# Where the projections of a backward kernel put their results: two PSUM banks instead of four, and one group made a stage earlier

## The chip, the core and the metric

The kernel runs on one core of one Trainium2 chip. The metric is the device time of one execution in microseconds (us); lower is better. The five engines are named as the profile names them: PE (TensorE, with its weight loads shown apart as PEld), DVE (VectorE), ACT (ScalarE), POOL (GpSimd) and SP (SyncE, which here only issues DMAs). PSUM is the memory that PE writes its results to; this kernel uses all eight of its banks.

## The reference: a gated mix of attention and a GLU, forward and backward

```python
x = A_x                                         # 1 x 2048 x 512
g = _sigmoid((x * gate_w).sum(-1, keepdims=True))
a = _A_ref(x, A_wqkv, A_wo)                     # 32 heads of 16, each row sees the last 256 keys
b = _B_ref(x, B_W_gate, B_W_up, B_W_down)       # relu(x Wg) * (x Wu), then Wd; inner width 1376
return g * a + (1 - g) * b
...
_out, _vjp = jax.vjp(_f, A_x, A_wqkv, A_wo, B_W_gate, B_W_up, B_W_down, gate_w)
_grads = _vjp(grad_out)
return (_out0, *[jnp.asarray(_g) for _g in _grads])
```

The outputs are the mix itself and its gradients with respect to the input and the six weights, in bfloat16.

## The kernel before: three stages, and an order of work that is written out by hand

**First stage** (lines 190 to 498): the GLU branch. Steps run over 11 blocks of 128 inner columns (`fc`) and, inside, over 4 groups of 512 tokens (`tg`), 44 steps in all (`N1`). A step makes gate and up products, the backward product `dh`, and six steps later (`at(6)`) the weight gradients (`weights`, lines 393 to 427). The loop runs 8 iterations past the last step, to empty this pipeline. In that tail the attention's first projections are slipped in: `first` holds the parts of token group 0, one popped per iteration (lines 489 to 493).

**Second stage** (lines 500 to 981): the attention, forward and backward together. The outer loop `c` runs over 4 chunks of 8 heads, the inner loop `j` over 16 blocks of 128 query tokens; for each query block up to three key blocks are visited, the diagonal one (role "d"), the one before (role "m") and the farthest (role "f"), each for two halves of four heads. One such visit is a unit; there are 90 units per chunk and 360 in all, and the loop variable `n` counts them. The order of instructions is written by hand (`manual_schedule`): every engine does its instructions in the order in which this loop issues them.

For unit `n`, `front` (line 666) makes the scores `ST` on PE, ACT takes their exponential into `Pu` (line 682), POOL masks it for roles d and f (lines 684, 687). `front_dp` (line 690) makes `dPT` on PE, and one step later `gradp` (line 698) multiplies the two on DVE. Three steps later `rowsum` (line 703) sums on PE into `BA`. Then the two results are turned over, `flip` (line 721): either by a DMA transpose issued on SP (line 729, all of role d, most of role m in the first three chunks), or by eight PE transposes into a PSUM tile `pt` and one copy on ACT or DVE (lines 734 to 741). The turned pairs feed `cd_piece` (line 524), which adds up the gradients of K and V in `CD`. `small_ops` (line 744) is the row arithmetic on POOL.

Beside the units, three kinds of work are put in by a running `credit` for PE's time (lines 866 to 965). First, `project_parts` (line 118) makes Q, dO, K, V for the next group of 512 tokens: the list `prq` of six parts (Q, dO, the DMA transpose `rows` of both, K, V, and the transposes `ptp` of K and V). Each of the four matmul parts has one PSUM tile `pp` of a whole bank, four matmuls and one reading copy; after Q and dO, four DVE copies `spread` (line 512) lay them out by heads. Second, `grad_parts` (line 613) makes the gradient of the projection weights of the chunk before: four sums per chunk, each a PSUM tile `wps` that stays open for four pieces of four matmuls (lines 621 to 632). Third, `late` and `early` issue loads and DMA transposes on SP for the last stage; `early` (line 784) holds one step that only makes a list and then four DMA transposes of the first 256 tokens' results.

**The PSUM banks of this stage.** Pool `ps` has four banks under the tag "M" and one for `CD`; pool `psr` has two under the tag "TR" and one for `BA`. Before, `ST`, `dPT`, `pp` and `wps` share the four "M" banks (line 511 sends the projections there), and `pt` and `ptp` have the two "TR" banks.

**SBUF pairs.** A d or m pair stays in a buffer `PPd` or `PPm`, three of each (line 677), until its DMA or PE transposes have read it. In the last chunk the pairs of query blocks 12 and 14 of role d are kept in `PPm` as well (line 675).

**Third stage** (lines 983 to 1090): for 8 pairs of token blocks, the output and the gradient of x, by long rows of 512-column matmuls. Its first groups use `T0` (from `early`), `f0` and `f1` (from `early_f`).

Of the kernel before, what the change touches and what calls it, by code (L numbers as in the profile page):

```python
# [11 lines left out]
BF = mybir.dt.bfloat16  # L12
F32 = mybir.dt.float32
# [9 lines left out]
def kernel(  # L23
# [88 lines left out]
    if True:  # L112
        HH = HG // 2
        proj = {}
        groups = [(c, tg) for c in range(DC) for tg in range(NTG)]
        PENG = ("dvs", "dvs")

        def project_parts(c, tg):
            t4 = {}
            proj[(c, tg)] = t4  # L120
            pj = pjA if (c * NTG + tg) % 3 == 0 else pjs["b"]

            def mm(nm, which, eng):
                ps, tag, bufs, _, _ = pools["now"]
                pp = ps.tile([P, TGW], F32, tag=tag, bufs=bufs, name="pp")
                for cd in range(DC):
                    if which < 3:
                        nc.tensor.matmul(pp[:], lhsT=w_p[c][:, cd, which * P:(which + 1) * P], rhs=x_T[tg][:, cd, :],  # L128
                                         start=(cd == 0), stop=(cd == DC - 1))
                    else:  # L130
                        nc.tensor.matmul(pp[:], lhsT=w_p[c][:, cd, 3 * P:4 * P], rhs=da_T[tg][:, cd, :],
                                         start=(cd == 0), stop=(cd == DC - 1))
                if nm in ("Q", "dO"):
                    if nm == "Q":
                        t4["z"] = pjA.tile([P, 2, TGW], BF, tag="zT", name="zT")
                    dst = t4["z"][:, ("Q", "dO").index(nm), :]
                else:
                    dst = pjA.tile([P, TGW], BF, tag="T", bufs=2, name=f"{nm}T")[:]
                if nm == "Q" and (c, tg) == groups[1]:
                    nc.scalar.mul(dst, pp[:], scale)  # L140
                elif nm == "Q":
                    nc.vector.tensor_scalar(dst, pp[:], scale, None, op0=ALU.mult)
                else:
                    evac(dst, pp[:], eng)
                t4[nm] = dst
                if nm in ("Q", "dO"):
                    if c == 0 and tg == 0:
                        w = ("Q", "dO").index(nm)
                        for k in range(NP):
                            rows = slice(32 * k, 32 * k + 32)  # L150
                            evac(zt[0][rows, w, k, :, :], dst[rows, :].rearrange("p (k q) -> p k q", k=TPG),
                                 (("dve", "act")[w] if k % 2 else "dve"))
                else:
                    for k in range(2):
                        t4[f"{nm}{k}"] = pj.tile([P, TGW], BF, tag=f"{nm}{k}", name=f"{nm}{k}")
                        if PENG[k] == "act":
                            nc.scalar.mul(t4[f"{nm}{k}"][:], pp[:], par[:, k:k + 1])
                        elif PENG[k] == "dve":
                            nc.vector.tensor_scalar(t4[f"{nm}{k}"][:], pp[:], par[:, k:k + 1], None, op0=ALU.mult)
                        else:  # L160
                            nc.vector.tensor_scalar(t4[f"{nm}{k}"][:], dst[:], par[:, k:k + 1], None, op0=ALU.mult)

            def tr(a_nm, b_nm):
                _, _, _, ps, trt = pools["now"]
                pt = ps.tile([P, 2, TPG, P], BF, tag=trt, bufs=2, name="ptp")
                for a, nm in enumerate((a_nm, b_nm)):
                    for k in range(TPG):
                        nc.tensor.transpose(pt[:, a, k, :], t4[nm][:, k * P:(k + 1) * P], ident[:])
                return pt

            def tr_rows():
                rows = pjA.tile([P, 2, TPG, P], BF, tag="rows", bufs=2, name="rows")
                nc.sync.dma_start_transpose(out=rows[:].rearrange("p a t d -> p (a t) d"),
                                            in_=t4["z"][:].rearrange("p a s -> p (a s)"))
                t4["rows"] = rows

            def tr_kv():
                kv = pj.tile([P, TPG, HG, 34], BF, tag="KV1", name="KV1")
                nc.gpsimd.memset(kv[:, :, :, 0:1], -1.0)
                nc.gpsimd.memset(kv[:, :, :, Dh + 1:Dh + 2], 1.0)  # L180
                pt = tr("K", "V")
                v = lambda a: pt[:, a, :, :].rearrange("p k (h d) -> p k h d", h=HG)
                nc.vector.tensor_scalar(kv[:, :, :, 1:1 + Dh], v(0), scale, None, op0=ALU.mult)
                nc.vector.tensor_copy(kv[:, :, :, Dh + 2:2 * Dh + 2], v(1))
                t4["kv"] = kv

            return [lambda: mm("Q", 0, "dve"), lambda: mm("dO", 3, "dve"), tr_rows, lambda: mm("K", 1, "act"),
                    lambda: mm("V", 2, "act"), tr_kv]

    with ExitStack() as p1, tc.manual_schedule():  # L190
# [248 lines left out]
        for n in range(N1 + 8):  # L439
# [51 lines left out]
            for _ in range({N1 + 1: 2, N1 + 2: 0}.get(n, 1)):  # L491
                if first:
                    first.pop(0)()
            z = n - DA0 - NT - 2
            if z == 0:
                load_w(0)
# [4 lines left out]
    if True:  # L501
# [6 lines left out]
        ps = pps.enter_context(tc.tile_pool(name="attps", bufs=2, space=PSUM))  # L508
        ppr = ExitStack()
        psr = ppr.enter_context(tc.tile_pool(name="attpr", bufs=2, space=PSUM, side="right"))  # L510
        pools["now"] = (ps, "M", 4, psr, "TR")
        def spread(gi, k):
            rows = slice(32 * k, 32 * k + 32)
            nc.vector.tensor_copy(zt[gi % ZB][rows, :, k, :, :].rearrange("p w t q -> p w (t q)"),
                                  proj[groups[gi]]["z"][rows, :, :])

        P2 = {}
        RQ = {}
        CDs = {}
# [93 lines left out]
        def grad_parts(c, tail=False):  # L613
            out = []
            hold = {}

            def store(part, ws):
                to = out_2[part * P:(part + 1) * P, :].rearrange("p (a n) -> p a n", a=3)[:, :, c * P:(c + 1) * P]
                return lambda: nc.sync.dma_start(to, ws[:])

            def piece(part, t0, first, last):
                if first:
                    hold[part] = ps.tile([P, 3, P], F32, tag="M", bufs=4, name="wps")
                wps = hold[part]
                for t in range(t0, t0 + 4):
                    nc.tensor.matmul(wps[:], lhsT=x_r[:, t, part * P:(part + 1) * P], rhs=sts[c][:, t, 0:3, :],  # L626
                                     start=first and t == t0, stop=last and t == t0 + 3)
                if not last:
                    return None
                ws = (S2["t6"] if tail else gwp).tile([P, 3, P], BF, tag="ws", bufs=5 if tail else 2, name="ws")  # L630
                evac(ws[:], wps[:], "act" if not tail or part % 2 else "dve")
                return store(part, ws)

            if tail:
                for a, b in ((0, NT - 4), (NT - 4, NT)):
                    out += [(p, t0, t0 == 0, t0 + 4 == NT) for p in range(DC) for t0 in range(a, b, 4)]
                return [lambda a=a: piece(*a) for a in out]
            for part in range(DC):
                for t0 in range(0, NT, 4):
                    out.append((lambda part=part, t0=t0, f=(t0 == 0), l=(t0 + 4 == NT): piece(part, t0, f, l), t0 + 4 < NT))  # L640
            return out
# [24 lines left out]
        def front(u):  # L666
# [5 lines left out]
            nc.tensor.matmul(ST[:], lhsT=KTt[:, ksl], rhs=z[:, 0, :, jl, :], start=True, stop=True)  # L672
            if not u.own:
                if u.half == 0:
                    kind = "m" if u.c == DC - 1 and u.j > 11 and u.j % 2 == 0 else u.role
                    tag = f"PP{kind}"
                    pairs[(u.c, u.j, u.kb)] = wk.tile([P, 2, 2, HH, P], BF, tag=tag, bufs=3, name=tag)
                u.PP = pairs[(u.c, u.j, u.kb)][:, u.half, :, :, :]
# [42 lines left out]
        def flip(u):  # L721
# [3 lines left out]
            if u.dma:  # L725
# [5 lines left out]
                for b in range(2)[hs]:  # L731
                    P2[(u.c, u.j, u.kb, b)] = P2[key][:, b, :, :, :]
                return
            eng = ("act", "dve")[copier["i"] % 2]
            copier["i"] += 1
            pt = psr.tile([P, 2, HH, P], BF, tag="TR", name="pt")
            for a, src in enumerate((u.Pu, u.Pd)):
# [99 lines left out]
        with tc.manual_schedule():  # L837
# [37 lines left out]
            while n <= NU + LAG or ev or cdq or bgq:  # L875
                now = ev.pop(n, [])
                u = units[n] if n < NU else None
                if u is not None:
# [2 lines left out]
                        sts[u.c] = st.tile([P, NT, 4, P], BF, tag="rows_st", name="rows_st")  # L881
                    if u.first and u.j % TPG == 0:
                        if gi + 1 < len(groups):
                            prq = project_parts(*groups[gi + 1])
                            due = n + sum(2 * min(3, j + 1) for j in range(u.j, u.j + TPG)) - 3
                            if gi + 2 == len(groups):
                                due -= 10
# [72 lines left out]
                if late and (u is None or u.c == 0 or (n % 12 == 1 and 3 <= u.j <= 8 if u.c < DC - 1 else  # L960
                                                       n % 4 == 1 and 1 < u.j < 10 or n % 2 and u.j > 9)):
                    late.pop(0)()
                if early and n % 3 == 0 and (len(early) > 4 or u is None or u.j >= 11):
                    early.pop(0)()
                credit = max(-1.0, min(1.2, credit))
                for eng, f in now:
# [154 lines left out]
```

## Time and profile before

| | us |
|---|---|
| median of 3 runs | 921.34 |
| the runs | 919.93, 921.34, 921.94 |
| the profiled execution, its own time | 921.62 |
| its span, first to last instruction | 919.9 |
| outside the span | 1.7 |
| PE busy in the span | 903.5 (98%) |
| DVE, ACT, POOL busy | 511.5, 437.8, 493.6 |
| first attention unit (its `ST`) starts | 249.74 |
| unit 18, the first of token group 1 | 270.76 |
| chunks 1, 2 and 3 start | 356.36, 473.90, 591.44 |
| the last unit's `ST` | 715.02 |

How to read it: all times inside the execution count from the start of the span. The PE busy time counts each matmul with a modelled end; a matmul of 512 columns is shown as 379 ns although the next one starts some 215 ns after it, so that short waits do not appear as idle time. The spacing of the starts in the timeline shows them.

### The profile page before, as it was taken

How to read it: one execution, taken by the hardware profiler on the slowest of the kernel's cores; microseconds unless marked ns; L12 is line 12 of the kernel's file. 1: busy time of each engine (PE TensorE's matmuls, PEld its weight loads, DVE VectorE, ACT ScalarE, POOL GpSimd, SP SyncE). 2: the span in 40 equal slices, each digit the busy share in tenths (PEclk: the TensorE clock that was granted, in tenths of full speed). 3: DMA queues.
4: the chain of work that ended last, by engine and by line, in shares of the span. 5: the costliest groups of instructions: out<-in, count | busy, mean ns of one | idle time of the engine just before them, and what ended most of it. 6: DMA issues, size and time to landing. Idle time of an engine off the chain costs nothing.

```text
span 919.9 us, 26221 instructions
## 1 busy us (share of the span) xinstructions
PE 903.5 (98%) x10711; PEld 569.7 (62%) x10711; DVE 511.5 (56%) x957; ACT 437.8 (48%) x773; POOL 493.6 (54%) x937
## 2 busy tenths in 40 slices
PE   9999999999999999999999999999998999999998
PEld 6556656556657776667666677766776644444445
DVE  4333344334288887668876687777786222222223
ACT  7322222222367777667776677766687300011111
POOL 4544445445277777767787677775777311111111
PEclk9999999999999999999999999999999999999999
DMA  9988889999699999998999989999999799777741
GB/s 303 193 195 188 190 179 215 221 222 194 159 164 157 179 182 187 191 164 149 171 196 187 162 158 182 184 179 185 181 187 197 184 255 234 183 188 184 184 93 46
DMA packets 505576, 169.07 MB, mean 184 GB/s; under 512 B 433456, under 2 KB 504336, under 8 KB 505456
## 3 DMA queue, kind: packets, MB, share of 16 engines
q1 hardware_dynamic: 484816, 145.51, 85.8%
q10 hardware_dynamic: 19008, 17.31, 6.9%
q0 software_dynamic: 1632, 4.59, 1.4%
q8 instruction: 83, 1.36, 0.6%
q14 instruction: 37, 0.30, 0.1%
HBM read 32.28 MB, written 36.24 MB: 74 GB/s over the span
## 4 chain that ended last, share of the span: by engine, by line
PE 79%; POOL 7%; DVE 4%; DMA 4%; issue 2%; ACT 2%; SPq 1%; ACTq 0%; POOLq 0%; DVEq 0%
PE dxps L1046 8%; PE ST L672 7%; PE dPT L696 7%; PE wps L403 7%; PE pt L739 5%; PE wps L626 4%; PE dxps L1050 4%; PE bps L1019 4%; PE pp L128 4%; PE CD L533 3%; PE BA L710 3%; PE dps L405 3%; PE ups L354 3%; PE gps L354 3%; PE dhps L354 3%
## 5 line engine op out<-in xcount | busy, mean ns | idle before, releaser
L696 PE MATMUL dPT<-z,V 128*128 128x512 bf16 x360 | 136.4, 379 | 3.7 <-ACT PPm L682 2.4
L672 PE MATMUL ST<-z,K 128*128 128x512 bf16 x360 | 136.3, 379 | 2.0 <-ACT PPm L682 0.3
L684 POOL TENSOR_SCALAR_AFFINE_SELECT PPd<-PPd 128x512 bf16<-128x512 bf16 x124 | 79.1, 638 | 106.9 <-ACT PPd L682 106.1
L701 DVE TENSOR_TENSOR Pd<-Pu,dPT 128x512 bf16<-128x512 bf16 x117 | 80.1, 684 | 64.7 <-POOL Pu L687 62.7
L368 POOL TENSOR_TENSOR hT<-rg,upm 128x512 bf16<-128x512 bf16 x44 | 51.5, 1171 | 116.1 <-DVE upm L366 90.0
L403 PE MATMUL wps<-dgu_r,x_r 128*128 128x256 bf16 (+1 forms) x704 | 103.9, 270 | 0.9 <-DVE wst L74 0.8
L701 DVE TENSOR_TENSOR PPd<-PPd,dPT 128x512 bf16<-128x512 bf16 x124 | 84.4, 680 | 15.5 <-POOL PPd L684 14.8
L403 PEld LDWEIGHTS <-x_r 128*128 128x128 bf16 x704 | 68.3, 98 | 31.9 <-issue 1.8
L682 ACT ACTIVATE PPd<-ST 128x512 bf16<-128x512 f32 x124 | 74.4, 600 | 27.3 <-PE ST L672 26.5
L682 ACT ACTIVATE PPm<-ST 128x512 bf16<-128x512 f32 x119 | 71.2, 601 | 29.9 <-PE ST L672 25.8
L682 ACT ACTIVATE Pu<-ST 128x512 bf16<-128x512 f32 x117 | 70.2, 600 | 28.9 <-PE ST L672 28.8
L701 DVE TENSOR_TENSOR PPm<-PPm,dPT 128x512 bf16<-128x512 bf16 x119 | 79.4, 667 | 6.5 <-POOL PPm L684 4.1
L687 POOL TENSOR_SCALAR_AFFINE_SELECT Pu<-Pu 128x512 bf16<-128x512 bf16 x112 | 73.7, 658 | 16.2 <-ACT Pu L682 15.6
L1026 ACT COPY a_sb<-aps 128x512 f32<-128x512 f32 x16 | 9.4, 586 | 151.4 <-issue 137.6
L366 DVE SCALAR_TENSOR_TENSOR upm<-rg,ups 128x512 bf16<-128x512 bf16 x44 | 30.1, 684 | 80.6 <-PE ups L354 44.2
L360 ACT ACTIVATE rg<-gps 128x512 bf16<-128x512 f32 x44 | 26.3, 598 | 88.4 <-PE gps L354 33.1
L405 PE MATMUL dps<-db_r,h_r 128*128 128x512 bf16 x176 | 66.7, 379 | 0.0
L72 ACT COPY p<-pt 128x1024 bf16<-128x1024 bf16 x62 | 63.0, 1016 | 5.2 <-PE dPT L696 0.4
L378 POOL TENSOR_TENSOR dgu<-dh_sb,rg 128x512 bf16<-128x512 bf16 x44 | 57.2, 1301 | 5.1 <-ACT dh_sb L374 5.1
L1032 POOL DMA_DIRECT2D out_dram<-o_sb x16 | 8.7, 542 | 89.2 <-DVE o_sb L1030 82.7
L128 PE MATMUL pp<-x,p 128*128 128x512 bf16 x192 | 49.0, 378 | 1.5 <-ACT PPm L682 1.0
L626 PE MATMUL wps<-rows_st,x_r 128*128 128x384 bf16 x256 | 50.3, 325 | 0.0
(193 smaller groups left out, 2362.3 us busy)
## 6 DMA issues: line engine op xcount, KB each, us to landing
dqkvo_d<-rows_st SPq DMA_DIRECT2D x15, 512.0 KB, 4.2
hT_d<-hT ACTq DMA_DIRECT2D x44, 128.0 KB, 2.5
dgT_d<-dgu ACTq DMA_DIRECT2D x44, 128.0 KB, 3.0
duT_d<-dgu ACTq DMA_DIRECT2D x44, 128.0 KB, 3.0
duT_g<-duT_d SPq DMA_DIRECT2D x8, 640.0 KB, 5.6
gt<-hT_d SPq DMA_DIRECT2D x7, 640.0 KB, 6.0
dgT_g<-dgT_d SPq DMA_DIRECT2D x7, 640.0 KB, 5.3
out_dram<-wst SPq DMA_DIRECT2D x20, 128.0 KB, 2.7
```

The source lines that it names most:

```text
L128: nc.tensor.matmul(pp[:], lhsT=w_p[c][:, cd, which * P:(which + 1) * P], rhs=x_T[tg][:, cd, :], start=(cd == 0), stop=(cd == DC - 1))
L354: nc.tensor.matmul(out[:], lhsT=w(c), rhs=x(c), start=(c == 0), stop=(c == DC - 1))
L403: nc.tensor.matmul(acc["w"][:, c, 0:2 * nw], lhsT=x_r[:, t, c * P:(c + 1) * P], rhs=k.dgu_r[:, :, i, s0:P], start=(go_ and c % 2 == 0), st ...
L405: nc.tensor.matmul(acc["d"][:], lhsT=k.h_r[:, i, :], rhs=db_r[:, t, :], start=go_, stop=no_)
L626: nc.tensor.matmul(wps[:], lhsT=x_r[:, t, part * P:(part + 1) * P], rhs=sts[c][:, t, 0:3, :], start=first and t == t0, stop=last and t == ...
L672: nc.tensor.matmul(ST[:], lhsT=KTt[:, ksl], rhs=z[:, 0, :, jl, :], start=True, stop=True)
L682: nc.scalar.activation(u.Pu[:], ST[:], ACT.Exp)
L684: nc.gpsimd.affine_select(out=u.Pu[:], in_=u.Pu[:], compare_op=ALU.is_ge, fill=0.0, base=0, pattern=[[0, HH], [1, P]], channel_multiplier=-1)
L687: nc.gpsimd.affine_select(out=u.Pu[:], in_=u.Pu[:], compare_op=ALU.is_ge, fill=0.0, base=-1, pattern=[[0, HH], [-1, P]], channel_multiplier=1)
L696: nc.tensor.matmul(u.dPT[:], lhsT=VTt[:, ksl], rhs=z[:, 1, :, jl, :], start=True, stop=True)
L701: nc.vector.tensor_tensor(out=u.Pd[:], in0=u.Pu[:], in1=u.dPT[:], op=ALU.mult)
L1046: nc.tensor.matmul(to, lhsT=src[:, fc, lsl], rhs=W6[(wt, fc)][:, cols], start=(fc == 0 and wt == "Wg"), stop=False)
```

## The change

The four parts of the change, as the code has them:

1. In the second stage `project_parts` takes its PSUM tiles from "TR" of `psr` instead of "M" of `ps`, and so do the `wps` sums of chunks 0 and 1 (made while chunks 1 and 2 run). The sums of chunks 2 and 3 stay in "M".
2. Q, dO and their `rows` transpose of token group 1 are made in the tail of the first stage, at its iterations `N1 + 4`, `N1 + 5` and `N1 + 6`, with the four `spread` copies right behind dO. `spread` moves up to where it can be called there, and the pool of the K and V buffers is looked up when a part runs. The attention's first group then has only K, V and their transposes left to put in.
3. In chunk 0 the copies of `pt` go ACT, DVE, ACT in turn, instead of ACT, DVE.
4. In the last chunk only query block 12's d pair is kept in `PPm`; block 14's goes to `PPd`. The list step of `early` may run from block 9 on, its four DMA transposes from block 14 on at even `n`; before, list and transposes ran at every third `n`, the transposes from block 11 on.

```diff
+        def spread(gi, k):
+            ...
         def project_parts(c, tg):
             t4 = {}
             proj[(c, tg)] = t4
-            pj = pjA if (c * NTG + tg) % 3 == 0 else pjs["b"]
+            pj = lambda: pjA if (c * NTG + tg) % 3 == 0 else pjs["b"]
...
+                    elif nm == "dO" and (c, tg) == groups[1]:
+                        for k in range(NP):
+                            spread(1, k)
...
             for _ in range({N1 + 1: 2, N1 + 2: 0}.get(n, 1)):
                 if first:
                     first.pop(0)()
+            if n == N1 + 3:
+                second = project_parts(*groups[1])
+            if n in (N1 + 4, N1 + 5, N1 + 6):
+                second.pop(0)()
...
-        pools["now"] = (ps, "M", 4, psr, "TR")
-        def spread(gi, k):
-            ...
+        pools["now"] = (psr, "TR", 2, psr, "TR")
...
             def piece(part, t0, first, last):
                 if first:
-                    hold[part] = ps.tile([P, 3, P], F32, tag="M", bufs=4, name="wps")
+                    own, tag, bufs = (ps, "M", 4) if c + 2 >= DC else (psr, "TR", 2)
+                    hold[part] = own.tile([P, 3, P], F32, tag=tag, bufs=bufs, name="wps")
...
-                    kind = "m" if u.c == DC - 1 and u.j > 11 and u.j % 2 == 0 else u.role
+                    kind = "m" if u.c == DC - 1 and u.j == 12 else u.role
...
-            eng = ("act", "dve")[copier["i"] % 2]
+            eng = ("act", "dve", "act")[copier["i"] % 3] if u.c == 0 else ("act", "dve")[copier["i"] % 2]
...
-                            prq = project_parts(*groups[gi + 1])
+                            prq = project_parts(*groups[gi + 1]) if gi else second
...
-                if early and n % 3 == 0 and (len(early) > 4 or u is None or u.j >= 11):
+                if early and (u is None or n % 2 == 0 and u.j >= (9 if len(early) > 4 else 14)):
                     early.pop(0)()
```

More of the change, by code (lines that the diff above doesn't have):

```diff
@@ L116 @@
         PENG = ("dvs", "dvs")
+        def spread(gi, k):
+            rows = slice(32 * k, 32 * k + 32)
+            nc.vector.tensor_copy(zt[gi % ZB][rows, :, k, :, :].rearrange("p w t q -> p w (t q)"),
+                                  proj[groups[gi]]["z"][rows, :, :])
         def project_parts(c, tg):
@@ L152, in mm @@
                                  (("dve", "act")[w] if k % 2 else "dve"))
+                    elif nm == "dO" and (c, tg) == groups[1]:
+                        for k in range(NP):
+                            spread(1, k)
                 else:
                     for k in range(2):
-                        t4[f"{nm}{k}"] = pj.tile([P, TGW], BF, tag=f"{nm}{k}", name=f"{nm}{k}")
+                        t4[f"{nm}{k}"] = pj().tile([P, TGW], BF, tag=f"{nm}{k}", name=f"{nm}{k}")
                         if PENG[k] == "act":
@@ L177, in tr_kv @@
             def tr_kv():
-                kv = pj.tile([P, TPG, HG, 34], BF, tag="KV1", name="KV1")
+                kv = pj().tile([P, TPG, HG, 34], BF, tag="KV1", name="KV1")
                 nc.gpsimd.memset(kv[:, :, :, 0:1], -1.0)
@@ L510 @@
         psr = ppr.enter_context(tc.tile_pool(name="attpr", bufs=2, space=PSUM, side="right"))
-        pools["now"] = (ps, "M", 4, psr, "TR")
-        def spread(gi, k):
-            rows = slice(32 * k, 32 * k + 32)
-            nc.vector.tensor_copy(zt[gi % ZB][rows, :, k, :, :].rearrange("p w t q -> p w (t q)"),
-                                  proj[groups[gi]]["z"][rows, :, :])
+        pools["now"] = (psr, "TR", 2, psr, "TR")
         P2 = {}
```

## The prediction, as it went on record

> **What bounds the kernel now.** I read the page's first and fourth parts, then the windows by stage, then the chain of waits and the timeline of the attention stage.
>
> ```profile
> span 919.9 us, 26221 instructions
> ...
> PE 903.5 (98%) x10711; PEld 569.7 (62%) x10711; DVE 511.5 (56%) x957; ACT 437.8 (48%) x773; POOL 493.6 (54%) x937
> ...
> PE 79%; POOL 7%; DVE 4%; DMA 4%; issue 2%; ACT 2%; SPq 1%; ACTq 0%; POOLq 0%; DVEq 0%
> ```
>
> PE is busy almost throughout and makes up 79% of the chain that ended last. What can be won is therefore the time in which PE starts nothing. Idle time hides most of that, because a matmul's end is modelled: the chain shows four 512-column matmuls as 0.86 us, 0.215 each, where the groups give 379 ns. So I went through PE's rows of the timeline from 249 to 710 us and took from each start-to-start distance what the matmul costs back to back (512 columns 0.215 us, 384 columns 0.163, a 128-column transpose 0.056, the small sums 0.025). The useful work comes to 437.1 us, the lost time to 22.9 us. All that follows is a share of these 22.9.
>
> The dearest single loss is near the end of the attention. The chain of waits there:
>
> ```profile
> 697.93 5.94 DMA p2d<-PPm
> 703.95 0.61 ACT PPm L682
> 704.60 0.38 PE dPT L696
> ```
>
> and the windows around it (PE busy, PEld, DVE, ACT, POOL, granted clock, DMA share, GB/s):
>
> ```profile
> 702.00:704.60 2.60, 0.23 (x3) 0.00 (x1) 0.18 (x1) 0.65 (x2) 0.00 (x0) 1.00 0.55 150
> ...
> 706.00:708.00 2.00, 2.00 (x28) 1.45 (x25) 1.40 (x4) 1.66 (x3) 1.75 (x5) 0.52 0.91 193
> 708.00:709.50 1.50, 1.50 (x28) 0.95 (x27) 0.53 (x1) 0.79 (x2) 1.18 (x4) 0.50 0.94 253
> ```
>
> The exponential of block 14's d pair must have a PPm buffer, and the next one free is that of block 12's pair, whose DMA transpose lands at 703.86. PE stands for 2.37 us, and then runs 3.5 us at half clock (0.52 and 0.50), 1.75 us more.
>
> The commonest loss is around a projection. The timeline (start, us, engine, line):
>
> ```profile
> 303.29 1.03 PE L131 MATMUL pp<-d,p 128*128 128x512 bf16 x4
> ...
> 304.36 0.69 DVE L74 CAST zT<-pp 128x512 bf16<-128x512 f32 x1
> 304.37 0.38 PE L696 MATMUL dPT<-z,V 128*128 128x512 bf16 x1
> ...
> 304.96 0.68 DVE L701 TENSOR_TENSOR PPd<-PPd,dPT 128x512 bf16<-128x512 bf16 x1
> 305.10 0.38 PE L672 MATMUL ST<-z,K 128*128 128x512 bf16 x1
> ```
>
> ST at 305.10 could not start until the cast had left pp's bank at 305.05; the eight BA sums before it were through at about 304.99. 21 of the 60 projection tiles in the attention are followed by such a wait.
>
> **End of the attention (block 14's pair to PPd).** PPd's three buffers then hold the pairs of blocks 11, 13 and 14, and 14 takes the one that block 10 left; that transpose was issued at 680.49 and landed at 686.20, 18 us before the need. Most that can come back: 2.37 + 1.75 = 4.1. Next late there is ACT, which in 712 to 716 is busy 3.89 of 4.00 us without holding PE up. I take 3.8.
>
> By the Trainium skill ("TensorE: Matmul & The Clock Gate", Part 1: The HAM clock gate) the clock halves only after an idle window of about 3.4 us. The 2.37 us of this trace were enough, so the trace decides; by the page the idle time alone, 2.4, would come back.
>
> **Projections out of the M banks.** From 271 us on (groups 2 to 15 in their making, 56 tiles) the lost time is 2.4 us before pp itself (mostly for an exponential to leave a bank), 2.4 before ST and dPT while a pp is open, and 2.3 before an ST that the copy out of pp released: 7.1 us, 0.13 a tile. With four banks for ST and dPT alone none of these waits has its cause left, but the DVE casts (0.69) and ACT casts (0.59) still stand in the same queues ahead of the products and exponentials that free the banks. Between 0 and 7.1 I take 60%, 4.3.
>
> What it costs in TR: I laid the life of every pt (129, mean 1.87 us from first transpose to end of copy), ptp (1.50), pp (1.72) and wps (6.88) of the trace over two banks. At no start are two others still alive; the tightest distances are 0.14 us (a wps at 396.2 and 513.7), and 0.57 for a pt behind a pt with wps open (397.3, 514.8). So 0; if the cover goes, see the third rival.
>
> **wps of chunks 0 and 1 to TR.** While a wps is open 0.97 us are lost before ST and dPT, in three chunks; two of them move: at most 0.65, I take 0.3.
>
> **Token group 1 in the first stage.** The tail before:
>
> ```profile
> 249.52 0.38 PE L405 MATMUL dps<-db_r,h_r 128*128 128x512 bf16 x1
> 249.74 0.38 PE L672 MATMUL ST<-z,K 128*128 128x512 bf16 x1
> 249.77 0.48 ACT L72 CAST wst_end<-wps 128x384 bf16<-128x384 f32 x1 [8.52 <-PE wps L403]
> ...
> 250.28 0.56 DVE L74 CAST wst_end<-wps 128x384 bf16<-128x384 f32 x1 [3.91 <-ACT wst_end L72]
> ```
>
> PE has no gap there (9.40 of 9.50 us busy from 240 to 249.5), so eight matmuls put the first ST off by 2 x 0.865 = 1.73, to about 251.5. Moved with them: the Q copy on ACT (0.60), covered, as ACT stands idle for 8.52; dO's cast (0.69) and four spreads (0.49 each, 1.96) on DVE, which come behind wst_end and before the first product, and hold that back to about 3.4 us after its ST instead of 2.3; one SP transpose (1.84), behind four stores (1.99) and ahead of the first p2d. The attention gives the 1.73 back, and the 2.65 on DVE. K, V and ptp move to n = 0, 2, 4, so units 5 to 17 run bare: they took 15.55 us with 2.2 of projection in them, and units 30 to 37, bare, 1.0 each, so 13.3. Units 0 to 4 take some 5.9 instead of 5.5 to n = 5. So 251.5 + 5.9 + 13.3 = 270.7, against 270.76. I take 0; the lost 4.4 us of this group and the 1.73 bound it at -2 and +2.
>
> **Copies in chunk 0.**
>
> ```profile
> L72 ACT COPY p<-pt x62: 1012/1012/1042, 262.8 to 718.7; 128x1024 bf16<-128x1024 bf16 x62
> L74 DVE COPY p<-pt x50: 676/684/692, 268.1 to 669.8; 128x1024 bf16<-128x1024 bf16 x50
> ```
>
> Of 28 copies 19 instead of 14 are ACT's: 5 x 1.01 = +5.1 on ACT, 5 x 0.68 = -3.4 on DVE. In chunk 0 ACT is busy 79.6 and DVE 86.6 of 106.7 us; they come level. 0, within 1 either way.
>
> **early later.** Its four transposes took SP 2.38 + 1.24 + 1.30 + 2.28 = 7.2 us between 682 and 697, ahead of block 12's and 13's p2d and the Wd loads. They now stand before block 14's and 15's p2d, f1 and wo. Cover: block 14's pair is used at 727.50, block 15's landed at 721.40 and is used at 728.30 (PE has 24 and more wps matmuls between), T0 is first read by aps at 733.81, f1 landed at 724.40 and is read at 734.67. If all 7.2 fell on block 15, with the attention 3.8 earlier: 724.8 against a need at 724.5, 0.3 lost. I take 0, at most 1.
>
> **Sum.** 3.8 + 4.3 + 0.3 = 8.4 off the profiled execution's 921.62 (span 919.9 and 1.7 around it): 913.2. That execution lies 0.28 above the median of the runs shown, 921.34; I put the forecast at 913.2. Bounds: all losses back 4.1 + 7.1 + 0.65 + 2 + 1 = 14.9, 906.7; only a part of the end back, 921.
>
> **Rivals.**
> 1. *The waits come back on ACT and DVE.* For: DVE is busy 70.0 of 85.6 us in the rest of chunk 0, and its largest wait, Pd for POOL's Pu, 62.7 us, stays. ST and dPT then wait for the late product instead of the bank, and only the end is gained: 921.6 - 3.8 = 917.8. Against: 2.3 us of the waits name pp's own copy. Chance 0.16.
> 2. *The change does not do what it says.* The first stage pays 1.73 and the DVE spreads delay the first units by the 2 bound; the end gains 3.8: 921.6 + 2 + 1 - 3.8 = 920.8, no change. For: PE has no gap in the tail. Chance 0.11.
> 3. *Slower: two TR banks become the narrow place.* In the overlay 18 starts that are new to these banks (pp, wps, or a pt behind one) come 0.14 to 0.60 us, 0.47 in the mean, after the bank is free. From the point where the copies end more than that later, PE waits there in order, with the next ST behind it. At 1 us later, one more ACT copy in front: 18 x 0.53 = 9.6 us, and the projections win nothing: 921.6 - 3.8 + 9.6 = 927.4. For: the copies queue behind exponentials on ACT at 1.01 us each, the longest pt lived 4.66. Against: the overlay. The Trainium skill ("Perfetto Trace Analysis", Optimizing Tensor Performance, Matmuls) asks that independent matmul groups rotate through different banks, so that one's copy overlaps the next; this speaks for this rival, and the overlay, with no collision in 129 flips, against it. Chance 0.15.
>
> The forecast (gain of 4 to 15) has 0.58. A measurement of this kernel tells 0.2%, 1.8 us, from no change. So faster: 0.58 + 0.16 = 0.74; within: 0.11; slower: 0.15. The range 907 to 921.5 takes the forecast with its bounds, the first rival and most of the second, and leaves out the third.
>
> **What the profile after would show.** End: no PE wait for ACT PPm near block 14, one p2d from PPm instead of two, granted clock 1.00 from 700 to 716. Projections: an ST within 0.03 us of the sums before it where a pp copy runs; no wait for DVE zT. TR: if pt, pp or wps wait for the copies of pt, the third rival holds. First stage: first ST near 251.5, unit 18 near 270.7. It would be wrong above all if PE's lost time between 271 and 700 us does not fall.

## The result: 913.5 us, 7 us less than before

| | before | after |
|---|---|---|
| median of the runs taken together | 920.63 (918.68 to 921.94) | 913.52 (912.6 to 913.66) |
| ratio, with its 95% interval | | 0.9922 [0.9902, 0.9943] |
| the profiled execution | 921.62 | 913.61 |

The forecast was 913.2. The head of the page and its shares of the chain that ended last, after:

```profile
span 911.9 us, 26209 instructions
...
PE 896.2 (98%) x10711; PEld 567.3 (62%) x10711; DVE 510.9 (56%) x952; ACT 441.6 (48%) x778; POOL 495.2 (54%) x937
...
PE 85%; POOL 6%; DVE 3%; DMA 2%; ACT 2%; issue 1%; SPq 1%; ACTq 0%; DVEq 0%; POOLq 0%
```

PE now makes up 85% of the chain instead of 79%, and still shows 98% busy: the page's busy share did not move, although the time lost in the attention, counted as in the prediction by the spacing of PE's starts, fell from 22.9 to 14.6 us.

Where the 8.0 us between the two profiled executions went is read best in stretches that begin and end with the same instruction. The first stage's own length differs by up to 2 us from run to run, so the sum begins with its last gate product (the first of the last four `gps` matmuls):

| stretch, us | before | after | change |
|---|---|---|---|
| start of the span to the last gate product | 225.56 | 225.27 | -0.29 |
| from there to the first `ST` | 24.18 | 26.68 | +2.50 |
| units 0 to 17 | 21.03 | 19.73 | -1.30 |
| units 18 to 89, the rest of chunk 0 | 85.60 | 85.71 | +0.11 |
| chunk 1 | 117.53 | 115.28 | -2.25 |
| chunk 2 | 117.54 | 115.44 | -2.10 |
| chunk 3, to the last `ST` | 123.58 | 118.06 | -5.52 |
| last `ST` to the end of the span | 204.90 | 205.74 | +0.84 |

The gain lies in chunks 1 to 3 (9.9 us). Three stretches that the prediction took as even gave 1.2, 1.4 (as an experiment will show, the +0.11 hides a gain and a loss) and 0.8 back.

The end of the attention after, in the windows that answer to those of before (PE, PEld, DVE, ACT, POOL busy, granted clock, DMA share, GB/s):

```profile
702.00:704.00 2.00, 2.00 (x40) 1.45 (x37) 1.97 (x4) 1.79 (x5) 1.92 (x5) 1.00 1.41 276
...
706.00:708.00 2.00, 2.00 (x57) 1.76 (x56) 1.06 (x2) 1.51 (x2) 2.00 (x5) 1.00 0.85 179
```

and the largest of PE's waits between 580 and 715 us (us in total, times, longest):

```profile
PE BA L720 <- DVE Pd L709: 0.4, 1, 0.4
```

The 2.4 us for ACT's `PPm` are gone, and the clock stays at 1.00 where it was 0.52.

A projection after (timeline: start, us, engine, line):

```profile
304.97 0.69 DVE L74 CAST zT<-pp 128x512 bf16<-128x512 f32 x1 [0.67 <-PE pp L136]
...
305.58 0.17 PE L720 MATMUL BA<-KV,PPm 128*128 128x17 bf16 x1
305.60 0.38 PE L680 MATMUL ST<-z,K 128*128 128x512 bf16 x1
```

Before, the `ST` behind dO's projection stood until the cast had left the bank. Now the cast runs from 304.97 to 305.66, and `ST` starts inside it, 0.02 us after the last `BA` sum.

### The profile page after: what moved, and what is told of

Its sections match the earlier page's. It is cut to its first block, busy times and chain, and to the rows that moved or that the text cites. A ratio compares the mean times of both kernels' runs of the same rounds, so it can differ in the third digit from the quotient of the medians.

```text
span 911.9 us, 26209 instructions
## 1 busy us (share of the span) xinstructions
PE 896.2 (98%) x10711; PEld 567.3 (62%) x10711; DVE 510.9 (56%) x952; ACT 441.6 (48%) x778; POOL 495.2 (54%) x937
## 4 chain that ended last, share of the span: by engine, by line
PE 85%; POOL 6%; DVE 3%; DMA 2%; ACT 2%; issue 1%; SPq 1%; ACTq 0%; DVEq 0%; POOLq 0%
PE wps L411 8%; PE dxps L1054 8%; PE ST L680 7%; PE dPT L704 7%; PE pt L747 5%; PE dxps L1058 4%; PE dps L413 4%; PE pp L133 4%; PE bps L1027 4%; PE ups L362 4%; PE dhps L362 4%; PE wps L634 4%; PE gps L362 4%; PE BA L718 4%; PE CD L540 4%; PE CD L543 2%
## 5 line engine op out<-in xcount | busy, mean ns | idle before, releaser
L72 ACT COPY p<-pt 128x1024 bf16<-128x1024 bf16 x67 | 68.3, 1020 | 3.8
L385 DVE TENSOR_TENSOR dgu<-dh_sb,upm 128x512 bf16<-128x512 bf16 x44 | 32.0, 727 | 32.7 <-ACT dh_sb L382 29.1
```

The costliest lines, as they stand in the source:

```text
L72: nc.scalar.copy(out, in_)
```

## Experiments

The theory was that of the prediction: the end of the attention and the banks of the projections bring the time, the rest is even. Its rivals were that DVE or ACT give the bank waits back, that two TR banks are too few, and, once the stretches of the changed kernel were seen, that three parts taken as nothing cost time. Four kernels made one part alone, four undid or varied one part of the changed kernel, and four started from the best parts. A median stands beside that of the kernel before on the same chip; a stretch is that of the one profiled execution. The ratios of experiments 5 to 8 (0.991 to 0.993, intervals of about 0.004) do not tell these kernels from the changed one (0.9922), so what is read from them rests on the stretches. Between the first `ST` and the last, stretches whose code a run leaves alone come out within 0.3 us of each other, but for chunk 3 where the stall near its end is kept; the stretch to the first `ST` varies by up to 0.5.

**1. The projections alone in TR** (before, with one line of the change)

```diff
-        pools["now"] = (ps, "M", 4, psr, "TR")
+        pools["now"] = (psr, "TR", 2, psr, "TR")
```

> The kernel before, with the projections' PSUM tiles in the two TR banks and nothing else changed. Bank theory (the wait for an M bank is the loss, and ACT and DVE have room): chunks 1 and 2, 117.54 us each before and 115.3 to 115.4 after the whole change, become 115.7 to 115.9, since the waits named for pp's copies are most of what went; chunk 3 wins about 1, chunk 0 at most 0.5, in all -5 us, 916. Engine theory (the waits come back at ACT and DVE): chunks 1 and 2 stay within 0.5 of 117.54, in all -1 or less. Narrow-TR theory: PE waits for the copies of pt and the time rises.

Measured: 916.29 against 920.73, ratio 0.9955 [0.994, 0.9969]. The rest of chunk 0 is 1.24 us shorter (84.36), chunks 1 and 2 by 1.45 and 1.49; units 0 to 17 take 0.36 more. There the trace names a wait that the kernel before does not have. By the code, the attention's first `pp` takes over a bank that the first stage used for `wps`, and it starts only when DVE has cast that into `wst_end`:

```profile
PE pp L128 <- DVE wst_end L74: 0.6, 1, 0.6
```

Chunk 3 is 0.29 longer, and the reason is the stall, which this kernel keeps. Its window and the one behind it:

```profile
694.50:698.30 3.80, 0.10 (x1) 0.00 (x0) 0.06 (x1) 0.54 (x2) 0.00 (x0) 0.76 1.18 174
698.30:703.40 5.10, 4.99 (x66) 3.61 (x66) 2.77 (x5) 4.00 (x7) 2.96 (x7) 0.51 0.95 188
```

PE stands 3.8 us instead of 2.4 and then runs 5 us at half clock instead of 3.4: what chunk 3 wins it loses again at its end. The banks' gain in chunk 3 can only be seen with the stall gone.

**2. The weight gradients of chunks 0 and 1 alone in TR**

```diff
-                    hold[part] = ps.tile([P, 3, P], F32, tag="M", bufs=4, name="wps")
+                    own, tag, bufs = (ps, "M", 4) if c + 2 >= DC else (psr, "TR", 2)
+                    hold[part] = own.tile([P, 3, P], F32, tag=tag, bufs=bufs, name="wps")
```

> The kernel before, with only the weight-gradient sums of chunks 0 and 1 moved to the TR banks. Bank theory: the PE waits with a wps open were 0.3 us a chunk, so chunks 1 and 2 fall by 0.3 to 0.5 each and nothing else moves, -0.6 to -1 in all. If instead the long-held wps is what crowds the M banks, chunks 1 and 2 fall by more than 1.5 each. Narrow-TR theory: flips wait and both chunks rise.

Measured: 919.62 against 920.73, 0.9988 [0.9972, 1.0004]. The times alone cannot tell it from nothing; the stretches can: chunks 1 and 2, where these sums are made, are 0.36 and 0.37 us shorter, and chunk 0 is as before (85.63). Together 0.7, a little over the bound of 0.65. Chunk 3 takes 124.81, 1.23 more, although nothing of it was changed: the stall at its end is 3.5 us long in this execution instead of 2.4. So its length is not fixed, and the times of kernels that keep it carry that too.

On top of experiment 1 the same part is worth more: chunks 1 and 2 take 116.09 and 116.05 with the projections alone in TR, and 115.36 and 115.37 with both (experiment 9), 1.4 together.

**3. Block 14's pair alone in PPd**

```diff
-                    kind = "m" if u.c == DC - 1 and u.j > 11 and u.j % 2 == 0 else u.role
+                    kind = "m" if u.c == DC - 1 and u.j == 12 else u.role
```

> The kernel before, with only block 14's diagonal pair of the last chunk kept in PPd. Theory: the stall of 2.37 us goes, and with it the 3.5 us at half clock, so chunk 3 up to its last ST falls from 123.58 to about 119.5, the granted clock reads 1.00 near its end, and the time falls by 4, to 917. Rival: the next holder of the pair buffers or ACT, busy 3.89 of 4 us there, makes PE wait again, and only 2 come back.

Measured: 917.03 against 920.73, 0.9959 [0.9945, 0.9974]. Chunk 3 goes from 123.58 to 119.76, 3.82 us; chunks 1 and 2 are unchanged to 0.01. The largest of PE's waits from 580 us to the last `ST` is now

```profile
PE dPT L696 <- DVE Pd L701: 0.8, 2, 0.5
```

as it stood behind the 2.4 us for ACT's `PPm` in the kernel before. The granted clock is 1.00 in every window of 2 us from 700 to 716.

**4. Token group 1 alone made in the first stage** (part 2 of the change as printed above, nothing else)

> The kernel before, with only Q, dO and rows of token group 1 made in the first stage. Theory after the trace of the changed kernel: the first ST starts 2.2 us later, since its PSUM bank is still read by dO's copy, and unit 18 stands 0.9 us later than before, so +0.9 us. Rival, that the attention's lighter first group pays for it: unit 18 at or ahead of 270.76, and 0 or less.

Measured: 922.54 against 920.73, 1.0016 [1.0004, 1.0027]: slightly slower. From the last gate product to the first `ST` 27.11 instead of 24.18, units 0 to 17 20.07 instead of 21.03; together 1.9 to 2.0 us more; the rest of chunk 0 is 0.25 shorter, and everything behind that as before. The timeline of the changed kernel shows the same place:

```profile
250.59 0.56 DVE L74 CAST wst_end<-wps 128x384 bf16<-128x384 f32 x1 [4.78 <-ACT wst_end L72]
251.12 0.69 DVE L74 CAST zT<-pp 128x512 bf16<-128x512 f32 x1
...
251.96 0.38 PE L680 MATMUL ST<-z,K 128*128 128x512 bf16 x1 [0.87 <-DVE zT L74]
```

`ST` of unit 0 does not read this `zT`; it is group 1's dO. By the code, it waits because dO's projection sits in one of the first stage's two "tr" banks, which the second stage's pools take over: until the cast has emptied it, the first `ST` has no place to write. And the cast stands behind `wst_end` in DVE's queue.

**5. The changed kernel without that part** (group 1 made in the attention, as before)

```diff
-            if n == N1 + 3:
-                second = project_parts(*groups[1])
-            if n in (N1 + 4, N1 + 5, N1 + 6):
-                second.pop(0)()
...
-                            prq = project_parts(*groups[gi + 1]) if gi else second
+                            prq = project_parts(*groups[gi + 1])
```

> The changed kernel with token group 1's Q, dO and rows back in the attention, the other parts kept. Theory: the first ST comes 2.2 us sooner and the first 18 units take about as long as the kernel before's 21.0 less the bank waits of the projections, some 20; unit 18 is 1 to 2 us sooner, and the time falls by 1 to 2 against the changed kernel. Rival, that the move pays once the projections are out of the M banks: the time rises.

Measured: 912.34 against 919.37, 0.9921 [0.9904, 0.9937]. From the last gate product to unit 18 it takes 45.55 us; the changed kernel and the two variants that share its first stage (6 and 7) take 46.41, 46.54 and 46.87. So inside the whole change the part costs 0.9 to 1.3 us.

**6. The changed kernel with copies of pt in turn, ACT, DVE, in chunk 0 too**

```diff
-            eng = ("act", "dve", "act")[copier["i"] % 3] if u.c == 0 else ("act", "dve")[copier["i"] % 2]
+            eng = ("act", "dve")[copier["i"] % 2]
```

> The changed kernel with the copies of chunk 0 alternating between ACT and DVE as before. Chunk 0 from unit 18 on took 85.60 us before and 85.71 after, although the projections left the M banks. Theory: little was lost there before, and the copies change nothing: 85.7 within 0.3. Rival: ACT's five more copies ate the gain, and the stretch falls to 85.0 or less.

Measured: 912.80 against 919.37, 0.9931 [0.9907, 0.9954]. The rest of chunk 0 takes 84.32 us instead of 85.71. The new order of the copies costs 1.4 us (by the spacing of the starts half of it, 0.7, stands before `dPT`, for DVE's product in `PPd`), and that is where chunk 0's gain from the banks (1.24 in experiment 1) went. "Nothing, within 1" fell.

**7. The changed kernel with `early` at its old places**

```diff
-                if early and (u is None or n % 2 == 0 and u.j >= (9 if len(early) > 4 else 14)):
+                if early and n % 3 == 0 and (len(early) > 4 or u is None or u.j >= 11):
```

> The changed kernel with the DMA transposes of early at their old places, from block 11 on at every third n. Theory: the 0.84 us that CD waits in the tail, for block 15's transposed pair, go, since those four no longer stand ahead of it on SP; from the last ST to the end 204.9 instead of 205.74, and nothing is lost near blocks 12 to 14, -0.8 in all. Rival: block 12's transpose lands late again and somebody near block 14 waits for it, 0 to +2.

Measured: 911.30 against 919.37, 0.991 [0.9891, 0.9929]. From the last `ST` to the end it takes 204.88 instead of 205.74 (206.13 and 206.14 in experiments 6 and 5, which keep the later places): 0.8 to 1.3 us. The profiled execution of experiment 8, which keeps them too, took 208.37, 3.5 more; the last section comes back to it. SP's queue of the changed kernel, and the wait of PE that it leads to:

```profile
708.91 1.31 SPq L802 DMA_TRANSPOSE early<-dqkvo_d  x1
...
714.16 2.89 SPq L737 DMA_TRANSPOSE p2d<-PPd  x1
```

```profile
PE CD L540 <- DMA p2d<-PPd: 0.7, 1, 0.7
```

One of `early`'s transposes and five other transfers (the rows of `dqkvo_d` and four loads of wo) stand ahead of block 15's turned pair, which is issued 8.0 us after the last `ST` (706.17) and lands at 14.1. `CD` would be ready for it at 13.3. With `early` at its old places the pair is issued 5.4 us after the last `ST` (706.81), lands at 10.5, and nobody waits for it:

```profile
712.23 3.04 SPq L737 DMA_TRANSPOSE p2d<-PPd  x1
```

**8. Group 1 one iteration earlier** (Q and dO at `N1 + 4`, the transpose at `N1 + 5`)

```diff
-            if n in (N1 + 4, N1 + 5, N1 + 6):
+            for _ in range({N1 + 4: 2, N1 + 5: 1}.get(n, 0)):
                 second.pop(0)()
```

> The changed kernel with Q and dO of token group 1 both put in before the last weight sums of the first stage, so that dO's copy and the spreads run beside those sums on DVE. Theory: the first ST no longer waits for dO's copy (1.04 us in the changed kernel) and the first products come sooner: first ST at 250.9, unit 18 sooner by 1.0 to 1.5, -1 to -1.5 us in all. Rival: the first units wait for something else, ACT's two stage-end copies or the masks, and less than 0.5 comes back.

Measured: 912.89 against 919.37, 0.993 [0.9906, 0.9954]. The wait of the first `ST` goes, as it should: 25.64 us after the last gate product instead of 26.68. But unit 18 comes after 47.34, no sooner than after 46.4 to 46.9:

```profile
253.85 0.58 ACT L72 CAST KT<-pp 128x512 bf16<-128x512 f32 x1 [2.04 <-DMA out_dram<-wst_end]
254.34 0.60 ACT L690 ACTIVATE PPd<-ST 128x512 bf16<-128x512 f32 x1
```

The next thing late is K's copy on ACT, which waits 2.04 us for the store of `wst_end`, and the exponential of `ST` behind it, for which a `dPT` stands 1.8 us. The wait has moved, and nothing is won.

**9. The two gains alone** (experiments 1, 2 and 3 together, on the kernel before)

> The kernel before with three edits of the change only: projections to TR, weight-gradient sums of chunks 0 and 1 to TR, block 14's pair to PPd. Left out: token group 1 in the first stage, the ACT-heavy copies of chunk 0, the later places of early. From the stretches of the earlier runs: chunk 0 from unit 18 on 84.35, chunks 1 and 2 115.3 each, chunk 3 118.0, last ST to the end 204.9; against the changed kernel -1.4 for the copies, -0.9 for early, -0.9 for the group, so 910.4, ratio to before 0.9890. Rival, that the parts left out were needed beside each other: no faster than the changed kernel.

Measured: 909.78 against 919.83, 0.99 [0.9879, 0.992], the lowest median of all. Units 0 to 17 21.39, the rest of chunk 0 84.35, chunks 1 to 3 115.36, 115.37, 118.01, and 204.89 behind the last `ST`. The intervals of the ratios of this kernel and the changed one (0.9922) overlap, so the times alone don't prove it the faster. The stretches do: 659.4 us from the first `ST` on against 660.0, and its first stage is that of before, 2.5 us shorter to the first `ST`. Chunk 3 is 1.75 shorter than in experiment 3: the gain of the banks that the stall had covered in experiment 1. (In the traces of experiments 9 to 12 a hundred matmul records of PE are missing, the same number in each; their lost time is therefore used only in differences between two of them.)

**10. As 9, the copies of chunk 0 DVE, ACT, DVE.** Experiment 6 left two causes: ACT's copy is the longer one (1.01 us against 0.68), or the change of places itself costs.

```diff
-            eng = ("act", "dve")[copier["i"] % 2]
+            eng = ("dve", "act", "dve")[copier["i"] % 3] if u.c == 0 else ("act", "dve")[copier["i"] % 2]
```

> The same three edits, and in chunk 0 two of three copies on DVE. If ACT's longer copy (1.02 us against 0.68) with the exponentials behind it is what cost 1.4 us in chunk 0, two of three on DVE lose nothing there: 84.0 to 84.6 from unit 18 on. If it is that any uneven turn puts two copies on one engine in one query block, the stretch rises to 85 or more here too.

Measured: 911.18 against 919.83, 0.9913 [0.9892, 0.9934]; the rest of chunk 0 takes 85.82 us instead of 84.35. Fewer copies on ACT cost as much as more of them (85.71), so the length of ACT's copy alone is not the cause.

**11. As 9, all copies of pt on ACT**

```diff
-            eng = ("act", "dve")[copier["i"] % 2]
+            eng = "act"
```

> The same three edits, and all copies of the PE transposes on ACT. It presses on the third rival of the prediction, that two TR banks become the narrow place once copies end later. ACT theory: the time rises by 5 to 15 us over the same edits without this one, and the PE waits stand before dPT and ST, for exponentials behind the copies. Narrow-TR theory: the waits stand before pt, pp, ptp and wps, for the copies themselves.

Measured: 916.28 against 919.83, 0.997 [0.9957, 0.9982]. The rest of chunk 0 86.33 (+1.98), chunks 1 to 3 +1.24, +1.22 and +1.12. The named waits of PE between 249 and 715 us hold none of a `pt`, `pp` or `wps` for a copy of `pt`; the largest two between 260 and 600 are

```profile
PE dPT L697 <- DVE PPm L702: 1.0, 3, 0.6
PE dPT L697 <- DVE PPd L702: 0.8, 3, 0.5
```

So even with every copy at 1.01 us the two TR banks do not hold PE up; what is named of the price stands before `dPT`. The shorter waits, which the modelled ends hide, say the same: by the spacing of the starts `dPT` loses 5.8 us in 37 places to DVE's product in `PPd`, against 0.5 us in 2 places in experiment 9. That is about the whole price of 5.6 us in the four chunks. This fits copies that keep ACT from the exponentials, so that the products come late, and with them the M banks. Also 0.8 us came up behind the last `ST` (205.73); that was not followed up.

**12. As 9, with the two engines exchanged in chunk 0**

```diff
-            eng = ("act", "dve")[copier["i"] % 2]
+            eng = ("dve", "act")[copier["i"] % 2] if u.c == 0 else ("act", "dve")[copier["i"] % 2]
```

> The three edits (projections and sums to TR, block 14's pair to PPd), and in chunk 0 the copies alternate the other way round: the first of a query block's two on ACT, the second on DVE. With ACT, DVE, ACT in turn chunk 0 from unit 18 on took 85.7, with DVE, ACT, DVE 85.8, with DVE and ACT alternating 84.35. If it is the unevenness (two copies in a row on one engine) that costs, 84.2 to 84.6 here as well. If it is the place (the first copy, close ahead of the second, belongs on DVE), 85.3 or more.

Measured: 912.35 against 920.55, 0.9914 [0.9883, 0.9944]; the rest of chunk 0 takes 87.01 us, 2.7 more, with 13 and 14 copies on the two engines as in 9. It is the place that counts. Each query block (six units) has two copies of pt. In turn, as in 9, the second comes 1.2 to 2.6 us after the first; the first is always DVE's and the second ACT's, and four blocks take 7.63, 8.22, 5.98 and 6.28 us; exchanged, 7.63, 8.40, 6.20 and 6.77, again and again. The last of these four, in the kernel of experiment 6, which alternates (its block begins at 292.36):

```profile
295.78 0.69 DVE L709 TENSOR_TENSOR Pd<-Pu,dPT 128x512 bf16<-128x512 bf16 x1 [0.89 <-POOL Pu L695]
295.89 0.60 ACT L690 ACTIVATE PPm<-ST 128x512 bf16<-128x512 f32 x1
...
296.39 0.68 DVE L74 COPY p<-pt 128x1024 bf16<-128x1024 bf16 x1
...
296.94 0.60 ACT L690 ACTIVATE PPd<-ST 128x512 bf16<-128x512 f32 x1 [0.45 <-PE ST L680]
```

and exchanged (its block begins at 292.06):

```profile
295.80 1.04 ACT L72 COPY p<-pt 128x1024 bf16<-128x1024 bf16 x1
...
296.71 0.64 ACT L683 ACTIVATE PPm<-ST 128x512 bf16<-128x512 f32 x1
296.85 0.69 DVE L702 TENSOR_TENSOR PPd<-PPd,dPT 128x512 bf16<-128x512 bf16 x1 [0.27 <-POOL PPd L685]
...
297.20 0.64 ACT L683 ACTIVATE PPd<-ST 128x512 bf16<-128x512 f32 x1
```

On DVE the first copy falls between `Pd` and a product for which POOL's mask is not ready: exchanged, DVE stands idle there (0.27 us). On ACT it falls ahead of two exponentials, and they come 1.1 and 0.6 us later in their block (4.65 instead of 3.53, 5.14 instead of 4.58). All on ACT (experiment 11) costs 1.98, where only the first copy has moved; the exchange costs 0.7 more, where the second has moved to DVE as well. What PE then waits for is only in part among the named waits (1.2 us before `CD` for `rq`, POOL's row arithmetic). By the spacing of the starts, less those of experiment 9, the stretch loses 1.1 us more before `CD` for `rq`, 0.8 before `ST` for ACT's exponential in `PPm`, and 0.8 before `dPT` for DVE's products; with small ones either way that is 2.6 of the 2.7.

## Why the prediction came out, point by point

The time was right, and of its parts one was right, one too small, and three that stood at nothing were not nothing. The gains were 2.4 us larger than forecast, the costs about 3.2 larger, and the two errors set each other off. With the one or the other alone put right the same sum would have given 911 or 916; that it came out within half a microsecond is luck.

- **End of the attention: -3.8 forecast, -3.82 measured** (experiment 3). Stall and half clock both went, and ACT, named as next, holds nothing up. The mechanism is shown; the 0.3 taken off the bound of 4.1 had no sum behind it, and experiment 2 shows that the stall itself varies (3.5 us instead of 2.4), so the agreement to the second digit is chance. By the rule of the Trainium skill ("TensorE: Matmul & The Clock Gate", Part 1: The HAM clock gate) it would have been the idle time alone, 2.4; the measurement stands against it.
- **Projections and weight gradients out of the M banks: -4.3 and -0.3 forecast.** From the kernel of experiment 9: -1.25 in the rest of chunk 0, -2.17 in chunks 1 and 2 each, -1.75 in chunk 3, +0.36 in units 0 to 17 (where experiment 1 names the wait for `wst_end`'s bank); -7.0 where -4.6 was taken. The step that failed is "between 0 and 7.1 I take 60%". From unit 18 on 7.3 of the 7.75 us that were laid to the two kinds of tiles came back. The projections alone account for 5.9 of their 7.1 (1.24, 1.45 and 1.49 in experiment 1, and the 1.75). The reason given for the discount, casts that still stand in the queues ahead of the products, does not show where the `zT` casts run: `ST` starts 0.02 us behind the sums, and after the first unit no `ST` waits for such a cast any more. The `wps` term, 0.3 with a bound of 0.65, was 0.7 alone and 1.4 with the projections moved too: with both gone the gain is larger than the two added up, which no part of the sum had.
- **TR: 0 forecast, next to 0 measured.** In the changed kernel one `pt`, in chunk 3, waits for a copy of another (`PE pt L747 <- DVE p2m L74: 0.2, 1, 0.2`). No `pp` or `wps` does, and with all copies on ACT no `pt` either. The overlay of lives had said so, with 0.14 us as its tightest distance.
- **Group 1 in the first stage: 0 forecast, +0.9 to +1.3 measured.** The 1.73 us of PE time were right, and so, nearly, were the shorter bare units (19.73 us for units 0 to 17, where 5.9 + 13.3 = 19.2 were forecast). The step missed is the bank: it was seen that dO's cast comes behind `wst_end` on DVE, but only the first product was put behind it, not the first `ST`, whose PSUM it empties (0.87 us). That put the first `ST` at 251.96 instead of 251.5, and unit 18 at 271.69 instead of 270.7. The first product, on the other hand, came 2.7 us after its `ST`, not 3.4. The bank is not the whole of it: with that wait gone (experiment 8) another took its place, and the cost stayed.
- **Copies in chunk 0: 0 forecast, within 1; +1.4 measured.** The step that failed is the balance of the two engines' busy time ("they come level"). It counted how many copies each engine has, and not which of a block's two copies; experiment 10 moved the balance the other way and cost the same.
- **`early` later: 0 forecast, at most 1; +0.8 to +1.3 measured, and +3.5 once.** Place, transfer and wait were named, and for the worst case a landing 13.6 us after the last `ST` (724.8 less 711.2) against a need at 13.3. The step that failed is taking 0 from a bound that lay on the need itself: the pair landed at 14.1, in experiments 5 and 6 at 14.5, and in the profiled execution of experiment 8 at 15.2. Without the move it lands at 10.5, so the cover is 2.8 us; the move issues it 2.6 later and takes 1.0 more from issue to landing (6.1 against 5.1), 3.6 in all. Without cover, every further delay of that landing is paid, once with a stretch at half clock on top.
- **Rivals.** The first (waits come back on ACT and DVE, 917.8) fell with chunks 1 and 2, which gained more than forecast; a piece of it is true in chunk 0, by way of the copies and not of the casts. Of the second (first stage pays, no gain, 920.8) the paying is true, at about half of the 2 us put on the first stage. The third (two TR banks too narrow, 927.4) has next to nothing for it: two banks for `pt`, `ptp`, `pp` and `wps` were enough. So the rule of the Trainium skill ("Perfetto Trace Analysis", Optimizing Tensor Performance, Matmuls) that was put beside it cost next to nothing here: the copies do overlap the next groups, with two banks as well.

Left open: what the rest of the change could be worth with the copies in turn and `early` at its old place, but group 1 in a bank of its own; no run tried it.

## What to carry to other kernels

The time that a mis-shared buffer cost came back nearly whole here when the other tiles left it, because the lives in the other pool, laid over each other, left room; the discount for engines that are merely busy was wrong. Before a piece of work is moved across a border of stages, ask what it holds (a PSUM bank, a staging buffer, a place in a queue) and who needs that first on the other side. And when a copy goes to the "freer" engine, look at what stands next in that engine's queue at that moment: here the gap it fits into decided, not the sums of busy time.

## What the runs showed of the hardware

An idle stretch of about 2 us can halve PE's clock, and need not. Experiment 8's profiled execution took 916.30 us, the other three of that kernel 912.2 to 912.9. It had a 1.8 us wait of `CD` in the tail, and behind it (windows, the clock is the third number from the right):

```profile
721.40:722.00 0.60, 0.56 (x17) 0.53 (x18) 0.00 (x0) 0.00 (x0) 0.00 (x0) 0.88 1.16 292
722.00:724.60 2.60, 2.60 (x9) 1.20 (x8) 0.71 (x3) 0.37 (x1) 0.96 (x1) 0.50 0.97 238
...
725.20:726.00 0.80, 0.80 (x7) 0.44 (x5) 0.33 (x1) 0.01 (x1) 0.00 (x0) 0.96 0.76 191
```

By the trace the half clock lasted from 721.86 to 725.27, 3.41 us. It lasted as long behind the stalls of 2.4 us (kernel before, experiment 4) and 3.5 us (experiment 2), and twice as long, 6.8 us, around the 3.8 us of experiment 1, where it began 1.9 us into the wait. So the price did not grow with the wait, but came in pieces of 3.4 us. Waits of 0.7 and 1.1 us in the tail (the changed kernel, experiments 5 and 6) left the clock at 1.00. So did longer ones elsewhere: 1.8 us at 253 in the same execution of experiment 8, and some 2 us in the first stage of the kernel before, the changed kernel and experiment 7. In the kernel before:

```profile
29.20:31.20 2.00, 0.05 (x1) 0.05 (x1) 0.07 (x1) 0.70 (x2) 1.89 (x2) 1.00 1.15 298
31.20:33.00 1.80, 1.80 (x9) 0.83 (x9) 0.96 (x2) 0.38 (x1) 1.47 (x2) 1.00 0.93 262
```

The length alone thus does not decide around 2 us; what else does, no run here shows. Where the clock fell, the wait cost more than its length: 208.37 us behind the last `ST` instead of 205.74, of which 1.1 is the longer wait, and the other 1.5 goes with the half clock.

Unexpected too was that the copies of the same 128 by 1024 elements, as many on each engine, cost 2.7 us more in the rest of chunk 0 when the two engines change places (experiments 9 and 12).
